# Attention steps in pairs, a later copy of the sine and cosine table, and one more empty step ahead of each batch's transforms

## The chip, the cores and the metric

The kernel runs on one core of a Trainium2 chip, in one launch. The metric is the device time of that launch in microseconds; the figure to forecast is the median of several executions. TensorE (PE in the rows) multiplies matrices, ScalarE (ACT) evaluates functions, copies and casts, VectorE (DVE) and GpSimd (POOL) work elementwise, and SyncE (SP) issues the DMAs. Each of them takes its instructions in program order.

## The reference

Three layers follow one another, in float32, over 4 batches, 448 positions and 768 features (12 heads of 64):

```python
# 1. attention with a sigmoid in place of the softmax
scores = q @ k.T / sqrt(64) - log(448)
x = sigmoid(scores) @ v                      # (4, 12, 448, 64) -> (4, 448, 768)
# 2. Fourier mixing, normalisation and a feed-forward network
u  = x + real(fft(fft(x, axis=1), axis=2))
un = (u - mean(u)) / sqrt(var(u) + 1e-6)
x  = u + relu(un @ w_ch1) @ w_ch2            # 768 -> 3072 -> 768
# 3. gated causal convolution
gate = sigmoid(conv(x, conv_w))              # 5 taps along the positions
out  = (gate * (x @ w_val)) @ w_out
```

## The kernel before

**Attention.** Heads go two at a time: 24 pairs of heads, 6 to a batch. Each pair takes four steps, one for each block of 128 keys (the fourth block, 64 keys of each head, is done for both heads in one). The main loop runs over the 96 steps `t`; `s = t % 4` is the block, `r` the step within the batch (24 to a batch). `scores(t)` (L355, L357) multiplies q and k in three matmuls (high by high, low by high, high by low halves) into one of two PSUM tiles `ps_s`; `sigmoid(t)` (L368, ScalarE) reads that tile; `values(t)` (L380, L382) multiplies its result with v in two passes and adds up in one `ps_m` tile over the four steps; `store_x` (L389, ScalarE) copies the sum out when `s == 3`.

For `s < 3` the scores of the two heads have 64 rows each and run side by side in the array: this shape is printed 64*128. Their values have 64 columns each and run side by side as 128*64. The fourth block and all other matmuls of this stage use the whole array, 128*128 (or some rows or columns less).

**Halves of q and k.** `prep_q` and `prep_k` cast the next pair's q and k (L308, ScalarE) and GpSimd subtracts for the low half (L309). Before, `prep_q` stands in the step with `s == 0` and `prep_k` in that with `s == 1`, both behind that step's sigmoid. The load of a further q or k waits until GpSimd has read the old one.

**One step.** In program order: scores of t+1, sigmoid of t, the casts, loads, then one step of each of the generators `fourier` (transforms of the batch before) and `norm` (normalisation of the one before that), a share of the step-wise weight preparation (`W_RATE` steps a step), then up to two ScalarE operations that those have queued (`drain`), then values and store of t-1. So the other matmuls stand between a scores and a values group.

**Tables.** The sine and cosine table `cs` comes in four parts through a staging tile (`cst`, tag `pm`, two buffers): its loads stand at r = 5, 6, 10, 11 of the first batch, its ScalarE copies at r = 8, 9, 14, 15. The first fold of a batch's transforms (`fold_part`, r = 19) uses the same two buffers. At r = 19 `peak_v` makes a 128x128 tile `pd` on VectorE, which a TensorE matmul (L117) reads at r = 21.

**Transforms.** `fourier(b)` starts at r = 2 of the next batch (the last batch's in the feed-forward stage). Its `main` waits some empty steps (`yield SLOT`), then `dstep` multiplies (L464, L468) the folded tiles `ph`, `pl`, and `mix` (L481) multiplies with `cs`. The yields counted before the first pair of `dstep` are 1 for b up to 2 and 4 for b = 3; before the second pair, 1.

**After attention** the feed-forward blocks `up` and `down` (L730, L753) take over; at each of their yields one step of what is left of `fourier`, `norm` and the weights is emitted. From there on nothing in the code is changed.

Of the kernel before, what the change touches and what calls it, by code (L numbers as in the profile page):

```python
# [7 lines left out]
F32 = mybir.dt.float32  # L8
# [9 lines left out]
B, H, S, D, DM, DFF = 4, 12, 448, 64, 768, 3072  # L18
# [19 lines left out]
G_EXP = -10  # L38
HALF_AT = (1, 3, 5, 6)
AHEAD = 7  # L40
LAG = 1
FOLD_AT = 18
WARM = 11
W_RATE = (1.6, 0.25, 1.25)
# [16 lines left out]
def body(tc, qd, kd, vd, w1d, w2d, cwd, wvd, wod, cdd, k12d, csd, eyed, out):  # L61
# [3 lines left out]
    def pool(stack, name, side="left"):  # L65
        return stack.enter_context(tc.tile_pool(name=name, bufs=1, side=side))
# [10 lines left out]
    wk = pool(attn, "wk")  # L77
# [211 lines left out]
    NHALF, NPAIR = 2 * B * H, B * NT  # L289
    raw, qk, st_of = {}, {}, {}  # L290
    SLOT = 1
# [10 lines left out]
    def halves_of(x, nm, n, on_v):  # L302
        h = wk.tile([128, n], F32R, tag=nm + "h", bufs=2, name=nm + "h")
        l = wk.tile([128, n], F32R, tag=nm + "l", bufs=2, name=nm + "l")
        if on_v:
            V.tensor_copy(h, x)
        else:
            A.activation(out=h, in_=x, func=AF.Copy)  # L308
        P.tensor_tensor(out=l, in0=x, in1=h.bitcast(F32), op=ALU.subtract)  # L309
        return h, l  # L310

    def prep_q(i):
        qk[i] = halves_of(raw[i][0], "q", S, i == 0)

    def prep_k(i):
        qk[i] += halves_of(raw.pop(i)[1], "k", 512, i < 3)
# [29 lines left out]
    def scores(t):  # L346
        i, s = divmod(t, 4)
        p = ps_s()
        qh, ql, kh, kl = qk[i]
        cs_ = slice(128 * s, 128 * s + 128)  # L350
        for n, (st, mv) in enumerate(((kh, qh), (kl, qh), (kh, ql))):
            if s < 3:
                for h in range(2):
                    hs = slice(64 * h, 64 * h + 64)
                    nc.tensor.matmul(p[:, h, :S], st[hs, cs_], mv[hs], start=(n == 0), stop=(n == 2))  # L355
            else:
                nc.tensor.matmul(p[:, 0, :S], st[:, cs_], mv, start=(n == 0), stop=(n == 2))  # L357
        if s == 3:
            qk.pop(i)
        sc[t] = p  # L360
# [3 lines left out]

    def sigmoid(t):
        n = width(t)
        sg = wk.tile([128, 2, S], F32, tag="sg", bufs=LAG + 2, name="sg")
        A.activation(out=sg[:, :n], in_=sc.pop(t)[:, :n, :S], func=AF.Sigmoid, scale=1.0 / math.sqrt(D), bias=logb)  # L368
        sig[t] = sg

    def values(t):
        i, s = t // 4, t % 4
        b, j = i // NT, i % NT
        if s == 0:
            xps[b, j] = ps_m()
        p, v, a = xps[b, j], vraw[b, j], sig.pop(t)
        if s < 3:
            for h in range(2):
                hs = slice(64 * h, 64 * h + 64)
                nc.tensor.matmul(p[hs, :S], v[:, s, hs], a[:, h], start=(s == 0), stop=False)  # L380
        else:
            nc.tensor.matmul(p[:, :S], v[:, s], a[:, 0], start=False, stop=True)  # L382
            vraw.pop((b, j))

    def store_x(t):
        i, s = t // 4, t % 4
        if s == 3:
            b, j = i // NT, i % NT
            A.activation(out=acc[b][:, j, PAD:], in_=xps.pop((b, j))[:, :S], func=AF.Copy)  # L389
# [10 lines left out]
    def fourier(b):  # L400
# [106 lines left out]
        def main():  # L507
            side.append(special())
            side.append(fold(0))
            while not hls or not rows:  # L510
                yield SLOT
            for _ in range(4 if b > 2 else 1):
                yield SLOT
            for c in range(2):
                yield from dstep(0, c, hls[0])
            side.append(fold(1))
            for h in range(2):
                nc.sync.dma_start(out=sp[h:6:2], in_=x[64 * h:64 * h + 1, 3:6])
            while len(hls) < 2:
                yield SLOT  # L520
            yield SLOT
            for c in range(2):
                yield from dstep(1, c, hls[1])
            while side:
                yield SLOT
            for _ in range(2 if b > 2 else 0):
                yield SLOT
            yield from mix(6, slice(64, NL, 64), add6)
            for t in range(3):
                yield from mix(128, slice(128 * t, 128 * t + 128), add(t))  # L530
# [105 lines left out]
    load_qk(3)  # L636
    nc.sync.dma_start(out=eye, in_=eyed)
    scores(0)
    mixed, cst, credit = {}, [], [0.0]
    for t in range(NHALF):  # L640
        i, g = t // 2, t % 2
        b = i // H
        r = t - b * 2 * H
        if t + 1 < NHALF:
            scores(t + 1)
        sigmoid(t)
        if t % 4 < 2 and t // 4 + 1 < NPAIR:
            (prep_k if t % 4 else prep_q)(t // 4 + 1)
        if t % 4 == 1 and t // 4 + 4 < NPAIR:
            load_qk(t // 4 + 4)  # L650
        if t % 4 == 1 and t // 4 + 2 < NPAIR:
            load_v(*divmod(t // 4 + 2, NT))
        if t == 0:
            amax_v(0, 0)
        if t % 4 == 2 and t // 4 + 1 < NPAIR:
            amax_v(*divmod(t // 4 + 1, NT))
        if r == 19:
            peak_v(b, 0)
        if r == 21:
            peak_v(b, 1)  # L660
        if r == 22:
            peak_v(b, 2)
            scale_v(b)
        if b and r == 2:
            fq.append(fourier(b - 1))
        step(fq)
        for n in range(3):
            if mixed.get(n) == 1:
                lq.append(norm(n))
            if n in mixed:  # L670
                mixed[n] += 1
        step(lq)
        if b == 0 and r in (6, 7, 8, 9):
            c, o = divmod(r - 6, 2)
            nc.sync.dma_start(out=cd[:, c, o], in_=cdd[:, c, o])
        if b == 0 and r == 12:
            nc.sync.dma_start(out=k12, in_=k12d)
        if b == 0 and r in (5, 6, 10, 11):
            c, o = divmod((5, 6, 10, 11).index(r), 2)
            cst.append(fk.tile([128, 3, 4 * NE], F32, tag="pm", bufs=2, name="cst")[:, :, :NP])  # L680
            nc.sync.dma_start(out=cst[-1], in_=csd[:, c, o])
        if b == 0 and r in (8, 9, 14, 15):
            c, o = divmod((8, 9, 14, 15).index(r), 2)
            push(out=cs[:, c, o], in_=cst.pop(0), func=AF.Copy)
        for n in range(2):
            if r == FOLD_AT + LAG + 4 * n:
                fold_part(b, n)
        if t > 6:
            credit[0] += W_RATE[0] if b == 0 else W_RATE[1] if r < 6 else W_RATE[2]
            step(wq, int(credit[0]))  # L690
            credit[0] %= 1
        drain(2 if t % 4 == 3 else 1)
        if t >= LAG:
            values(t - LAG)
            store_x(t - LAG)
    for t in range(NHALF - LAG, NHALF):
        values(t)
        store_x(t)
    drain()
    finish(wq)  # L700
    attn.close()
# [182 lines left out]
    for part, n in blocks:  # L884
        g, b = n // B, n % B
# [177 lines left out]
```

## Time and profile before

| | |
|---|---|
| Median of 3 runs | 1081.32 us (1080.78 to 1081.84) |
| Profiled execution: own time | 1081.04 us |
| Profiled execution: span | 1079.2 us |
| Mean granted TensorE clock | 0.995 of full speed |
| TensorE busy | 1058.7 us, 98% |
| VectorE, ScalarE, GpSimd busy | 739.2, 444.4, 180.3 us |
| Attention ends (last values matmul) | about 225.3 us from the span's start |

The span runs from the first to the last instruction; 1.84 us of the execution's own time lie around it. A busy TensorE is not a TensorE at its peak: the end of a matmul is modelled, so that a later start of the next one is seen in the distance between two starts, and only a long one as idle time.

### The profile page before, as it was taken

What the parts mean: (1) busy time and instruction counts of PE and PEld (TensorE: products, weight loads), DVE (VectorE), ACT (ScalarE), POOL (GpSimd) and SP (SyncE); (2) the same over time, 40 slices, a digit from 0 to 9 for tenths busy, and PEclk for the clock granted to TensorE, in tenths of its full rate; (3) what the DMA queues carried; (4) which work ended last, traced back from release to release, by engine and by line L of the source; (5) the groups of instructions that cost most, each with busy time, mean ns of one, the idle gap of its engine ahead of it and who ended that gap; (6) DMA issues with size and microseconds to landing.
All of it is one profiled execution on the core that took longest, in us unless ns stands there. A gap on an engine that the chain in (4) does not pass through costs nothing. (4 is left out here: it accounts for less than half of the span.)

```text
span 1079.2 us, 15323 instructions
## 1 busy us (share of the span) xinstructions
PE 1058.7 (98%) x5616; PEld 548.9 (51%) x5616; DVE 739.2 (68%) x2143; ACT 444.4 (41%) x686; POOL 180.3 (17%) x162
## 2 busy tenths in 40 slices
PE   9999999999899999999999999999999999999998
PEld 5345454546455555555555555555555545555554
DVE  2866999696985666667676566666666787776530
ACT  5675757732232233333233333133333374444321
POOL 3322223200020112211021122012221061000000
PEclk9999999999999999999999999999999999999999
DMA  6632432011112322223322222322222200000001
GB/s 218 211 94 88 130 97 88 11 46 45 30 30 59 83 64 69 78 60 88 89 75 72 60 74 72 89 73 60 73 71 76 60 1 1 1 35 35 35 35 69
DMA packets 34780, 74.13 MB, mean 69 GB/s; under 512 B 3940, under 2 KB 11920, under 8 KB 34704
## 3 DMA queue, kind: packets, MB, share of 16 engines
q1 hardware_dynamic: 34704, 73.15, 23.7%
q8 instruction: 44, 0.72, 0.3%
q14 instruction: 32, 0.26, 0.1%
HBM read 67.46 MB, written 5.51 MB: 68 GB/s over the span
## 5 line engine op out<-in xcount | busy, mean ns | idle before, releaser
L730 PE MATMUL ps_s<-un,w1hi 128*128 128x448 f16 x1152 | 312.8, 353 | 2.0 <-DVE hl L739 2.0
L753 PE MATMUL ps_m<-hh,w2hi 128*128 128x448 f16 x576 | 203.5, 353 | 3.6 <-DVE acc L757 2.4
L753 PE MATMUL ps_m<-hh,w2lo 128*128 128x448 f16 x576 | 203.6, 353 | 0.0
L753 PE MATMUL ps_m<-hl,w2hi 128*128 128x448 f16 x576 | 203.4, 353 | 0.0
L730 PE MATMUL ps_s<-un,w1lo 128*128 128x448 f16 x576 | 203.4, 353 | 0.0
L753 PEld LDWEIGHTS <-w2hi 128*128 128x128 f16 x1152 | 112.4, 98 | 109.4 <-issue 5.0
L730 PEld LDWEIGHTS <-w1hi 128*128 128x128 f16 x1152 | 112.9, 98 | 108.3 <-issue 4.1
L757 DVE SCALAR_TENSOR_TENSOR acc<-ps_m,rg,acc 128x448 f32<-128x448 f32 x192 | 129.1, 680 | 36.8 <-PE ps_m L753 36.6
L178 ACT ACTIVATE wabs<-w 128x384 f32<-128x384 f32 (+1 forms) x109 | 58.4, 547 | 223.9 <-DMA w<-w2d 81.1
L739 DVE SCALAR_TENSOR_TENSOR hl<-ps_s,hh 128x896 f16<-128x896 f32 x64 | 54.7, 855 | 80.0 <-ACT hh L737 79.9
L189 DVE TENSOR_SCALAR_CACHE_REDUCE wabs<-wabs 128x192 f32<-128x192 f32 (+1 forms) x234 | 74.7, 354 | 41.7 <-ACT wabs L178 40.7
L368 ACT ACTIVATE sg<-ps_s,logb 128x896 f32<-128x896 f32 x96 | 86.5, 912 | 26.8 <-PE ps_s L355 22.6
L753 PEld LDWEIGHTS <-w2lo 128*128 128x128 f16 x576 | 56.4, 98 | 53.0 <-issue 0.7
L730 PEld LDWEIGHTS <-w1lo 128*128 128x128 f16 x576 | 56.5, 98 | 52.8 <-issue 0.4
L191 DVE TENSOR_SCALAR wf<-wabs 128x192 int32<-128x192 int32 (+1 forms) x234 | 54.4, 272 | 35.6 <-POOL w1lo L230 13.2
L929 PE MATMUL ps_m<-xs,wvhi 128*128 128x448 f16 x288 | 78.0, 352 | 0.0
L197 DVE SCALAR_TENSOR_TENSOR wf<-w,wf 128x192 int32<-128x192 int32 (+1 forms) x234 | 77.3, 369 | 0.3
L737 ACT ACTIVATE hh<-ps_s 128x896 f16<-128x896 f32 x64 | 46.1, 720 | 73.6 <-PE ps_s L730 73.6
L194 DVE SCALAR_TENSOR_TENSOR wf<-w,wf 128x192 int32<-128x192 int32 (+1 forms) x234 | 74.6, 357 | 0.3
L380 PE MATMUL ps_m<-sg,v 128*64 128x448 f32 x288 | 70.3, 568 | 0.0
L810 DVE SCALAR_TENSOR_TENSOR gp<-acc,cw,gp 128x448 f32<-128x448 f32 x72 | 49.3, 685 | 20.3 <-ACT gp L808 18.4
L954 PE MATMUL ps_m<-gh,wohi 128*128 128x448 f16 x144 | 50.8, 352 | 0.0
(185 smaller groups left out, 1399.1 us busy)
## 6 DMA issues: line engine op xcount, KB each, us to landing
w<-w1d SPq DMA_DIRECT2D x42, 384.0 KB
w<-w2d SPq DMA_DIRECT2D x42, 384.0 KB
k<-kd SPq DMA_DIRECT2D x24, 256.0 KB
v<-vd SPq DMA_DIRECT2D x24, 256.0 KB
q<-qd SPq DMA_DIRECT2D x24, 224.0 KB
out<-o SPq DMA_DIRECT2D x24, 224.0 KB
w<-wvd SPq DMA_DIRECT2D x12, 384.0 KB
w<-wod SPq DMA_DIRECT2D x12, 384.0 KB
```

The source lines that it names most:

```text
L178: A.activation(out=wa, in_=z[:, :, 1].bitcast(F32), func=AF.Abs)
L189: V.tensor_scalar(out=a, in0=a, scalar1=LEAST, scalar2=None, op0=ALU.max, op1=ALU.max, accum_out=m[:, i:i + 1])
L191: V.tensor_scalar(out=f.bitcast(I32), in0=a.bitcast(I32), scalar1=0x07FFFFFF, scalar2=3, op0=ALU.bitwise_and, op1=ALU.logical_shift_left)
L194: V.scalar_tensor_tensor(out=f.bitcast(I32), in0=lo, scalar=29, in1=f.bitcast(I32), op0=ALU.logical_shift_right, op1=ALU.bitwise_or)
L197: V.scalar_tensor_tensor(out=f.bitcast(I32), in0=hi, scalar=-0x40000000, in1=f.bitcast(I32), op0=ALU.bitwise_and, op1=ALU.bitwise_or)
L368: A.activation(out=sg[:, :n], in_=sc.pop(t)[:, :n, :S], func=AF.Sigmoid, scale=1.0 / math.sqrt(D), bias=logb)
L380: nc.tensor.matmul(p[hs, :S], v[:, s, hs], a[:, h], start=(s == 0), stop=False)
L730: nc.tensor.matmul(p[:, i, :S], w[:, k, fs], u[:, k], start=(m == 0), stop=(m == 17))
L739: V.scalar_tensor_tensor(out=l[:, :nf], in0=p[:, :nf, :S], scalar=0.0, in1=h[:, :nf], op0=ALU.max, op1=ALU.subtract)
L753: nc.tensor.matmul(p[:, :S], w[:, f, js], hh[f // 2][k][:, f % 2], start=(m == 0), stop=(m == 3 * FC - 1))
L757: V.scalar_tensor_tensor(out=acc[b][:, j, PAD:], in0=p[:, :S], scalar=rg, in1=acc[b][:, j, PAD:], op0=ALU.mult, op1=ALU.add)
L929: nc.tensor.matmul(p[:, :S], w[:, k, js], u[:, k], start=(n == 0), stop=(n == 17))
```

## The change

The order of the work in the attention loop is changed. In every even step the scores of two steps (t+2 and t+3) are issued one after the other and then their two sigmoids; in every odd step the values of two steps (t-1 and t). The other matmuls of a step now stand ahead of both. `prep_q` and `prep_k` stand together in the step with `s == 0`, ahead of that step's scores. The number of sigmoid buffers goes from 3 to 4. Two of the four table loads move from r = 10, 11 to 13, 14, the copies from 8, 9, 14, 15 to 10, 11, 18, 19. Each `fourier` gets one empty step more ahead of its first pair of `dstep` (not in the last batch) and one more ahead of the second.

```diff
-LAG = 1
-        sg = wk.tile([128, 2, S], F32, tag="sg", bufs=LAG + 2, name="sg")
+        sg = wk.tile([128, 2, S], F32, tag="sg", bufs=4, name="sg")
 ...
-            for _ in range(4 if b > 2 else 1):
+            for _ in range(4 if b > 2 else 2):
                 yield SLOT
 ...
             while len(hls) < 2:
                 yield SLOT
+            yield SLOT
             yield SLOT
 ...
     scores(0)
+    scores(1)
+    sigmoid(0)
+    sigmoid(1)
 ...
-        if t + 1 < NHALF:
-            scores(t + 1)
-        sigmoid(t)
-        if t % 4 < 2 and t // 4 + 1 < NPAIR:
-            (prep_k if t % 4 else prep_q)(t // 4 + 1)
+        if t % 4 == 0 and t // 4 + 1 < NPAIR:
+            prep_q(t // 4 + 1)
+            prep_k(t // 4 + 1)
 ...
-        if b == 0 and r in (5, 6, 10, 11):
-            c, o = divmod((5, 6, 10, 11).index(r), 2)
+        if b == 0 and r in (5, 6, 13, 14):
+            c, o = divmod((5, 6, 13, 14).index(r), 2)
 ...
-        if b == 0 and r in (8, 9, 14, 15):
-            c, o = divmod((8, 9, 14, 15).index(r), 2)
+        if b == 0 and r in (10, 11, 18, 19):
+            c, o = divmod((10, 11, 18, 19).index(r), 2)
             push(out=cs[:, c, o], in_=cst.pop(0), func=AF.Copy)
 ...
-            if r == FOLD_AT + LAG + 4 * n:
+            if r == FOLD_AT + 1 + 4 * n:
                 fold_part(b, n)
 ...
         drain(2 if t % 4 == 3 else 1)
-        if t >= LAG:
-            values(t - LAG)
-            store_x(t - LAG)
-    for t in range(NHALF - LAG, NHALF):
-        values(t)
-        store_x(t)
+        if g == 0 and t + 2 < NHALF:
+            for n in (t + 2, t + 3):
+                scores(n)
+            for n in (t + 2, t + 3):
+                sigmoid(n)
+        if g:
+            for n in (t - 1, t):
+                values(n)
+                store_x(n)
```

## Rows read from the trace of the kernel before

**Rows 1.** The page, part 1: busy time, share of the span, instructions of each engine.
```profile
PE 1058.7 (98%) x5616; PEld 548.9 (51%) x5616; DVE 739.2 (68%) x2143; ACT 444.4 (41%) x686; POOL 180.3 (17%) x162
```

**Rows 2.** Busy time by stretch (start:end, length, engines, clock, DMA): three later batches, two short ones.
```profile
...
50.12:108.00 57.88, 56.85 (x316) 28.89 (x316) 38.46 (x99) 37.62 (x56) 14.53 (x12) 1.00 0.32 101
108.00:166.00 58.00, 56.74 (x317) 29.36 (x313) 55.17 (x124) 38.32 (x56) 17.13 (x13) 1.00 0.37 108
166.00:225.30 59.30, 57.57 (x318) 30.19 (x315) 50.13 (x114) 40.02 (x58) 14.40 (x11) 1.00 0.14 42
...
38.00:41.00 3.00, 3.00 (x11) 1.12 (x10) 2.67 (x8) 2.99 (x6) 1.57 (x2) 0.50 0.54 173
...
280.00:290.00 10.00, 7.44 (x29) 3.30 (x28) 9.93 (x24) 0.95 (x1) 0.41 (x1) 0.84 0.13 32
```

**Rows 3.** TensorE in order of time, one step in the loop: start, length, instruction.
```profile
11.90 0.47 PE L355 MATMUL ps_s<-qh,kh 64*128 64x448 f32 x2
12.21 0.36 PE L355 MATMUL ps_s<-qh,kl 64*128 64x448 f32 x2
12.41 0.37 PE L355 MATMUL ps_s<-ql,kh 64*128 64x448 f32 x2
12.71 0.97 PE L380 MATMUL ps_m<-sg,v 128*64 128x448 f32 x4
13.61 0.48 PE L355 MATMUL ps_s<-qh,kh 64*128 64x448 f32 x2
```

**Rows 4.** TensorE in order of time, groups of one shape behind each other.
```profile
7.00 0.37 PE L355 MATMUL ps_s<-ql,kh 64*128 64x448 f32 x2
7.21 0.38 PE L355 MATMUL ps_s<-qh,kh 64*128 64x448 f32 x2
7.41 0.38 PE L355 MATMUL ps_s<-qh,kl 64*128 64x448 f32 x2
...
222.85 1.72 PE L380 MATMUL ps_m<-sg,v 128*64 128x448 f32 x8
...
224.51 1.02 PE L382 MATMUL ps_m<-sg,v 128*128 128x448 f32 x2
```

**Rows 5.** Order of time, ScalarE, TensorE and SyncE around the table copy of r = 14.
```profile
35.18 0.52 ACT L259 ACTIVATE cs<-cst 128x384 fp32r<-128x384 f32 x1 [3.04 <-DMA cst<-csd]
...
36.27 0.47 PE L355 MATMUL ps_s<-qh,kh 64*128 64x448 f32 x2 [1.90 <-ACT sg L368]
...
29.87 0.43 SPq L681 DMA_DIRECT2D cst<-csd  x1
...
35.08 0.39 SPq L322 DMA_DIRECT2D v<-vd  x1
```

**Rows 6.** Order of time, VectorE and TensorE around the first batch's peak of v.
```profile
45.38 0.29 DVE L111 TENSOR_SCALAR pd<-eye,vt 128x128 fp32r<-128x128 f32 x1
...
47.26 0.33 PE L117 MATMUL ps_m<-pd,ones_r 128*128 128x128 f32 x1
```

**Rows 7.** Groups by line, 0 to 225.3 us: count, busy, mean ns, idle before.
```profile
L308 ACT ACTIVATE qh<-q 128x448 fp32r<-128x448 f32 x23 | 13.1, 569 | 0.0
...
L309 POOL TENSOR_TENSOR kl<-k,kh 128x512 fp32r<-128x512 f32 x24 | 31.7, 1321 | 50.7 <-ACT kh L308 48.4 <-DMA q<-qd 1.9 <-DVE kh L306 0.4
L309 POOL TENSOR_TENSOR ql<-q,qh 128x448 fp32r<-128x448 f32 x24 | 29.2, 1218 | 91.3 <-ACT qh L308 88.5 <-DVE qh L306 2.8
```

**Rows 8.** ScalarE in order of time: one copy-out of a finished pair of heads.
```profile
15.48 0.55 ACT L389 ACTIVATE acc<-ps_m 128x448 f32<-128x448 f32 x1 [1.12 <-PE ps_m L382]
```

**Rows 9.** What TensorE waited for, 0 to 225.3 us: total, times, longest.
```profile
PE ps_s L355 <- ACT sg L368: 4.9, 7, 1.9
```

**Rows 10.** Order of time, TensorE, ScalarE, VectorE: waits around the transforms, end of attention.
```profile
126.84 0.70 PE L464 MATMUL ps_m<-cd,pl 128*113 128x385 f16 x3 [0.91 <-DVE pl L436]
...
181.03 0.67 ACT L259 ACTIVATE e<-eo,st 12x452 f16<-12x452 f32 x1 [3.01 <-DVE eo L417]
...
223.11 1.08 DVE L618 TENSOR_TENSOR un<-tt,un 128x896 f16<-128x896 f32 x1
```

## The prediction

> **What bounds the kernel now.** I read the page's busy times first: TensorE is busy for 98% of the span, VectorE for 68%, ScalarE for 41% [rows 1]. Work that TensorE does not have to do, or that it does closer together, shortens the time, unless another engine sets the pace of that stretch. The change lies in the attention stage, so I looked next at that stage's batches in the view by stretch [rows 2]. TensorE is busy nearly throughout, but in the third batch (108 to 166 us) VectorE is busy for 55.17 of 58.00 us, in the fourth for 50.13 of 59.30, in the second for 38.46 of 57.88. The reader is to keep that third batch in mind. Last I read the order of time on TensorE, by the distance from one start to the next, since a late start does not show as idle time.
>
> A step [rows 3] has its three score matmuls start at 11.90, 12.21 and 12.41 and its values at 12.71: distances of 0.31, 0.20 and 0.30, in all 0.81 us for the scores; the values take until 13.61, 0.90 us; the step 1.71. Where two scores groups of the same shape stand behind each other [rows 4], the last matmul of the first (7.00) and the first of the second (7.21) both take 0.20 to 0.21. So a change of shape costs about 0.1 us at the end of a scores group and 0.1 at its start. Two values groups behind each other take 222.85 to 224.51, 1.66 us, against 2 x 0.90 = 1.80 apart.
>
> **The change part by part.**
>
> *Pairs.* A pair of heads now has eight changes of array shape, in the new order six: the scores of s = 0 and 1 stand together, and so do the values of s = 0 and 1. The other two neighbours (s = 2 and 3) differ in shape and save nothing. Two scores groups together take 0.31 + 4 x 0.20 + 0.30 = 1.41 instead of 1.62, which saves 0.21; the values save 0.14; 0.35 us for a pair of heads. The first two scores and the last two values already stand together [rows 4], so there are 23 of each: 23 x 0.35 = 8.05, which I count as **-8.1**. Other matmuls between two groups add a change of shape when both neighbours are of split shape. That was so at s = 1 and s = 3 and is now so at s = 2 and s = 3: two places of four either way, counted at nothing.
>
> The exits (0.30 instead of 0.20) [rows 3] fit what the Trainium skill states in "TensorEngine Tiling (Array Packing)", Key Properties: a change of the tiling mode drains TensorE. By that rule alone, only the drain would be saved, 46 removed changes at the 0.10 of the exit, an estimate of 4.6 us. The rows show the entry as well, and I take the rows.
>
> *Table copies.* The third load of the table was issued at 29.87, its copy began at 35.18, 5.3 us later; ScalarE waited 3.04 us for it, the sigmoid behind it came late and TensorE idled 1.90 us [rows 5]. From 38 to 41 us the granted clock was 0.50, the lower level, which costs half of those 3.0 us, 1.5: 3.4 us in all. The load now stands behind those of q, k and v at r = 13, the last of which SyncE issued at 35.08 [rows 5]: so about 35.5, and with the same 5.3 us it lands at about 40.8. ScalarE comes to the copy when the sigmoid of step 19 is done. Step 4 starts at 11.90 [rows 3]; a pair of heads takes 4 x 1.71 - 0.35 = 6.5; step 20 would start at about 38, and that sigmoid ends a little before, at about 37. So the later place does not by itself remove the wait, 3.8 us instead of 3.0. What changes is how much of it reaches TensorE: from 38.1 it has two scores (1.41) and the values of s = 2 and 3 to do (0.90, and 0.95 for the full-array group, whose row is 0.05 longer, 1.02 against 0.97; 1.85), until 41.4; the copy (0.5) and the next sigmoid (1.0) end at 42.3. That is 0.9 us idle, and 0.1 more for the second sigmoid.
>
> Next late is `pd`: VectorE finished it at 45.38 + 0.29 = 45.67 and TensorE read it at 47.26 [rows 6]. Its place in VectorE's queue is behind weight preparation that waits for DMAs, and those stand in SyncE's queue behind loads of q and k that GpSimd must free first, later than now since the casts stand behind the store. Two table loads less in the crowded stretch work the other way. I take 45.7 (45.0 to 47.5 are possible). TensorE then does this matmul 1.6 us earlier than before, with one more scores group (0.81) behind it: 2.4 us gained by then, of which five pairs of heads at 0.35 are 1.75. The table and `pd` together: **-0.6** (from -3.4, both waits gone, to +1.5).
>
> *Casts.* `prep_q` and `prep_k` now follow the copy-out of the finished pair of heads (0.55) [rows 8] on ScalarE. From the start of that copy the low half of k takes 0.55 + 0.57 (cast of q) + 1.22 + 1.32 (the two GpSimd subtractions, q first) [rows 7] = 3.66 us. The first matmul to read it comes after two scores (1.62), two values (1.66) and one matmul (0.31), 3.59 us. With the hand-overs and a weight load that can no longer be prefetched it is some 0.25 us late where nothing else stands between, and hidden where other matmuls do. Those of `fourier` and `norm` run in some 15 of the 24 pairs of heads by the order in the code; in the first batch the wait for `pd` absorbs it. Five pairs of heads are left: **+1.2** (0 to 6, 0.25 in all 24).
>
> *Empty steps.* TensorE waited 0.91 us in a transform for a low half from VectorE [rows 10]. One step ahead is worth 1.7 us, so this wait and smaller ones of the kind go: **-1.0** (0 to -1.5).
>
> *ScalarE's waits.* TensorE waited 4.9 us for sigmoids, 1.9 of them at the table [rows 9]; 3.0 are left in six waits. The largest followed ScalarE's 3.01 us wait for the transform's `eo` [rows 10]. Now two sigmoids are done ahead, and such an operation behind them has the 1.66 + 1.41 + 1.85 us of three pairs of groups, less itself and the next sigmoid: some 2.5 us of room. I take **-1.2** (0 to -3.0).
>
> *VectorE.* Against this stands that VectorE's work does not shrink. The third batch would be 2.1 us shorter (six pairs of heads), 55.9 us with 55.17 of VectorE work [rows 2]. I let a little over half of that batch's saving go: **+1.2** (0 to +4.2, the fourth batch too).
>
> *After attention.* Two empty steps more push the last of `norm`, such as the 1.08 us operation at 223.11 [rows 10], behind the start of the feed-forward blocks, and the last `fourier` starts a step or two later. There VectorE can be the bound: from 280 to 290 us it is busy for 9.93 us and TensorE for 7.44 [rows 2]. **+0.8** (-1 to +2.5).
>
> The fourth sigmoid buffer costs no time that a row shows; start and end of the loop are within the terms above.
>
> **The sum.** -8.1 - 0.6 + 1.2 - 1.0 - 1.2 + 1.2 + 0.8 = -7.7 us. The profiled execution's own time is 1081.04 us (span 1079.2 and 1.84 around it), so 1073.3; it lies 0.3 below the median of 1081.32, for which the forecast is 1073.6.
>
> **The rivals.**
>
> *VectorE takes most of it back.* If the third and fourth batch run at VectorE's pace, they keep none of their 2 x 2.1 us. What is left is the first batch (1.75 + 0.6) and the second (2.1), less the 0.8 after attention: 3.7 us, 1077.6. For it: 55.17 of 58.00 us. Against it: the fourth batch has 9 us of room, and the waits of TensorE for VectorE are short now.
>
> *The cast chain makes it slower.* In the new order a whole pair of heads lies between the copy-out and the next use of k, and the chain already fills it (3.66 against 3.59). If a queued ScalarE operation (0.67 for `e`) [rows 10] stands before the copy-out each time, some 0.6 us is lost in each of 24 pairs, 14.4 us. The other terms sum to -8.9, so it decides from 0.37 us for a pair of heads on; at 0.6 the time is 1081.3 + 5.5 = 1086.8. Against it: such an operation runs while TensorE is still at the 1.85 us of values before the copy, and ScalarE is busy for only 38.32 of 58.00 us in the fullest batches [rows 2].
>
> *The distance isn't a matter of shape.* If the extra 0.1 us belonged to every first and last matmul of a group, whatever stands beside it, standing together would save nothing; the rest sums to about -0.4 with the casts' and VectorE's terms smaller too: 1081. Two groups of one shape behind each other speak against it [rows 4].
>
> **How the numbers follow.** I give my forecast 0.63, VectorE 0.20, the casts 0.07, no effect of the shape 0.10. All the favourable bounds together would give 8.1 + 3.4 + 1.5 + 3.0 + 1.0 = 17.0 us, 1064.3; I do not expect all of them at once and set the low end at 1068.0. The high end of 1080.5 takes in VectorE's case and part of the one without effect, and leaves out the casts'. Within 0.2% (1079.2 to 1083.5) is about what a measurement of this kernel can't tell from no change. Faster than that: 0.79 (the forecast, most of VectorE's case); within it: 0.14; slower: 0.07.
>
> **What the new profile would show.** Right: scores groups of s = 0 and 1 with no 0.3 us distance between them, two values groups in 1.66 us, attention ended at about 218 us, and ScalarE's wait for `cst` still there with TensorE's idle time behind it halved. `pd` is then read almost as soon as it is made. Wrong: a TensorE wait for GpSimd at the second scores matmul of most pairs of heads (casts); VectorE full to the brim from 108 to 220 us with TensorE waiting at L464, L596 or L117 (VectorE); distances of 0.3 us inside the new pairs (shape); or an end of attention that is early and a feed-forward stage that starts no earlier, its first waits on VectorE longer by as much.

## The result and the profile after

The changed kernel takes 1091.95 us (median of 4 runs, 1090.02 to 1092.62) against 1081.05 us (4 runs, 1079.33 to 1081.84): a ratio of 1.0102, 95% interval 1.0088 to 1.0115. It is slower by about 11 us where 7.7 us less were forecast. The profiled execution's own time is 1090.02 us, its span 1088.2. Part 1 of its page, to set beside [rows 1]:

```profile
PE 1054.4 (97%) x5616; PEld 553.9 (51%) x5616; DVE 740.7 (68%) x2143; ACT 444.6 (41%) x686; POOL 184.2 (17%) x162
```

The work is the same and TensorE is even busy for 4 us less; what grew is the time in which it stands. Attention ends (first feed-forward matmul) at 227.72 us, before at 225.36; from there to the end of the span it takes 860.52 us, before 853.87. So the profiled execution lost 2.4 us in attention and 6.6 us behind it, 9.0 in all (it lies 1.9 us below the median, so some 2 of the 11 us are not in this account). The 6.6 were lost before 420 us: from the 433rd matmul of `up` on, the kernel before needs 670.28 us and this one 669.75. The batches by stretch, to set beside [rows 2] (length, then PE, PEld, DVE, ACT, POOL, clock, DMA):

```profile
52.20:109.10 56.90, 56.17 (x318) 30.87 (x316) 37.75 (x98) 37.24 (x56) 15.66 (x12) 0.98 0.36 110
109.10:168.30 59.20, 55.59 (x317) 30.93 (x317) 54.45 (x130) 37.87 (x55) 18.32 (x13) 1.00 0.35 105
168.30:227.70 59.40, 56.09 (x312) 30.51 (x309) 47.67 (x98) 39.75 (x58) 14.85 (x11) 1.00 0.12 36
49.00:53.00 4.00, 4.00 (x13) 1.53 (x14) 3.83 (x12) 0.00 (x0) 0.00 (x0) 0.50 0.38 112
240.00:250.00 10.00, 7.86 (x35) 4.23 (x35) 9.87 (x32) 2.96 (x5) 0.00 (x0) 0.83 0.16 42
```

The second batch is 1.0 us shorter than before, the third 1.2 us longer, though VectorE works no more in it. TensorE in order of time at a new pair of scores:

```profile
18.70 0.47 PE L354 MATMUL ps_s<-qh,kh 64*128 64x448 f32 x2
19.04 0.47 PE L354 MATMUL ps_s<-qh,kl 64*128 64x448 f32 x2
19.35 0.36 PE L354 MATMUL ps_s<-ql,kh 64*128 64x448 f32 x2
19.55 0.37 PE L354 MATMUL ps_s<-qh,kh 64*128 64x448 f32 x2
19.76 0.36 PE L354 MATMUL ps_s<-qh,kl 64*128 64x448 f32 x2
19.96 0.37 PE L354 MATMUL ps_s<-ql,kh 64*128 64x448 f32 x2
20.26 0.97 PE L379 MATMUL ps_m<-sg,v 128*64 128x448 f32 x4
```

Between the two groups (19.35, 19.55, 19.76) the distance is 0.20 to 0.21, as forecast; the 0.31 behind the second line (19.04 to 19.35) is that of the first reader of `kl`, which GpSimd had finished only at 18.99. Summed over TensorE's starts from 6 us to the end of attention, what the distances at changes of shape hold beyond those of one shape fell from 36.0 us (204 changes) to 28.0 us (157). The other late starts rose from 10.2 to 20.1 us. This is a reckoning, and where one draws the line between a change of shape and another late start moves each of these differences by 1 to 2 us. What TensorE waited for in attention (total, times, longest):

```profile
PE ps_s L354 <- ACT sg L367: 4.0, 4, 1.6
PE ps_s L354 <- POOL kl L308: 4.0, 8, 1.0
PE ps_m L116 <- DVE pd L110: 3.6, 1, 3.6
```

The second and third lines are new: TensorE begins at 48.62 to read a `pd` that VectorE finished at 48.56, and the clock's lower level lasts until 54 us. So is a chain through four queues at the start of the third batch; here it is in order of time, engine by engine:

```profile
112.71 0.33 SPq L297 DMA_DIRECT2D q<-qd  x1
114.32 0.33 SPq L298 DMA_DIRECT2D k<-kd  x1
114.70 0.42 SPq L321 DMA_DIRECT2D v<-vd  x1
115.17 1.42 SPq L551 DMA_DIRECT2D acc<-sp  x2
...
117.88 1.29 DVE L564 TENSOR_TENSOR tt<-tt,acc 128x448 f32<-128x448 f32 x2 [2.57 <-DMA acc<-sp]
...
125.29 0.67 ACT L258 ACTIVATE e<-eo,st 12x452 f16<-12x452 f32 x1 [4.82 <-DVE eo L416]
...
127.05 0.47 PE L354 MATMUL ps_s<-qh,kh 64*128 64x448 f32 x2 [1.64 <-ACT sg L367]
```

The same write-back in the kernel before:

```profile
107.01 1.43 SPq L551 DMA_DIRECT2D acc<-sp  x2
```

With the two empty steps (one ahead of each half of a batch's transforms), `fourier(0)` ends in step r = 1 of the third batch, whose q, k and v loads are written ahead of it; before, it ended in the last step of the second. SyncE's 257 issues stand in the order of the code. The q load leaves when GpSimd has read the old q (`ql` runs from 111.54 to 112.69), the k load when `kl` is done (112.64 to 114.29), and the write-back `acc<-sp` behind them at 115.17. VectorE stands at the norm's addition L564 for 2.57 us, ScalarE waits 4.82 us for `eo` made behind it, a sigmoid comes late, and TensorE idles 1.64 us. The same happens in the fourth batch (1.57 us at L564, 1.26 us on TensorE).

Behind attention, in order of time on VectorE and TensorE:

```profile
233.04 1.09 DVE L618 TENSOR_TENSOR un<-tt,un 128x896 f16<-128x896 f32 x1 [1.92 <-ACT un L258]
236.00 0.62 DVE L564 TENSOR_TENSOR tt<-acc 128x448 f32<-128x448 f32 x1
...
241.00 1.08 DVE L743 SCALAR_TENSOR_TENSOR hl<-ps_s,hh 128x896 f16<-128x896 f32 x1
...
242.14 0.90 PE L734 MATMUL ps_s<-un,w1hi 128*128 128x448 f16 x2 [4.04 <-DVE hl L743]
```

The last L618 of `norm(1)` begins 5.3 us past the end of attention; before, it began 2.3 us ahead of it [rows 10]. `norm(2)` begins (first L564) 8.3 us past it, before 0.2 us ahead. TensorE's idle time from attention's end to the 433rd feed-forward matmul is 15.2 us, before 7.9.

### The profile page after: what moved, and what is told of

The parts are those of the page before. It is cut to its first block, busy times and chain, and to the rows that moved or that the text cites. A ratio compares the mean times of both kernels' runs of the same rounds, so it can differ in the third digit from the quotient of the medians.

```text
span 1088.2 us, 15324 instructions
## 1 busy us (share of the span) xinstructions
PE 1054.4 (97%) x5616; PEld 553.9 (51%) x5616; DVE 740.7 (68%) x2143; ACT 444.6 (41%) x686; POOL 184.2 (17%) x162
## 4 chain that ended last, share of the span: by engine, by line
PE 79%; DVE 11%; issue 5%; DMA 2%; POOL 1%; ACT 1%; SPq 0%; ACTq 0%; POOLq 0%; DVEq 0%
PE ps_m L757 28%; PE ps_s L734 27%; PE ps_m L933 8%; PE ps_m L958 8%; PE ps_m L379 2%; PE ps_s L354 2%; PE ps_m L463 2%; DMA w<-w1d 1%; PE ps_m L480 1%; POOL kl L308 1%; DVE acc L761 1%; PE ps_m L381 1%; DVE un L582 1%; PE ps_s L356 1%; DVE gp L835 1%
## 5 line engine op out<-in xcount | busy, mean ns | idle before, releaser
L761 DVE SCALAR_TENSOR_TENSOR acc<-ps_m,rg,acc 128x448 f32<-128x448 f32 x192 | 129.7, 681 | 47.5 <-PE ps_m L757 47.2
L367 ACT ACTIVATE sg<-ps_s,logb 128x896 f32<-128x896 f32 x96 | 82.4, 911 | 51.8 <-PE ps_s L354 51.4
L379 PE MATMUL ps_m<-sg,v 128*64 128x448 f32 x288 | 66.2, 568 | 0.0
L308 POOL TENSOR_TENSOR ql<-q,qh 128x448 fp32r<-128x448 f32 x24 | 30.0, 1249 | 141.8 <-ACT qh L307 139.0
```

Of the source, the lines that this page charges most:

```text
L761: V.scalar_tensor_tensor(out=acc[b][:, j, PAD:], in0=p[:, :S], scalar=rg, in1=acc[b][:, j, PAD:], op0=ALU.mult, op1=ALU.add)
```

## The experiments

Seventeen kernels ran. A line of a diff stands against the kernel after unless said otherwise.

### Which part costs

No empty steps:

```diff
-            for _ in range(4 if b > 2 else 2):
+            for _ in range(4 if b > 2 else 1):
 ...
-            yield SLOT
             yield SLOT
             for c in range(2):
                 yield from dstep(1, c, hls[1])
```

> The changed kernel without its two extra empty steps ahead of the transforms; pairs, casts and table as changed. Theory 'empty steps': they push the last additions of the third batch's transforms and the last normalisation steps behind the start of the feed-forward blocks, where VectorE is late by 4.2 us instead of 2.1; the stalls from the end of attention to about 345 us are 20.4 us in the changed kernel and 13.1 before, so this kernel should be 5 to 7 us faster than the changed one, about 1085 us (some 1 to 2 us of waits for pl come back). Theory 'casts' (the late low half of k delays attention, and VectorE's lateness follows from that): the time stays within 2 us of the changed kernel, 1090 to 1092.

1082.99 us, ratio 1.0019 (1.0010 to 1.0028): 9.0 us of the 11 are the empty steps', more than the 5 to 7 expected. From attention's end it takes 853.56 us, as before.

The kernel before with the two empty steps alone (the same lines added):

> The kernel before with only the two extra empty steps. Theory 'empty steps': 4 to 7 us slower than before, 1085 to 1088 us, lost behind the end of attention, with a first wait for hl of about 4 us. Theory 'casts': the empty steps cost nothing without the new order, 1081 us, and the wait for pl at 126 us (0.9 us) is gone.

1094.85 us, ratio 1.0128 (1.0105 to 1.0152). Without pairs the steps cost even more, 13.6 us, about twice what I expected: in the profiled execution 5.0 in attention, where TensorE's waits for sigmoids grow from 4.9 to 9.4 us, and 9.0 behind it.

The table's loads and copies at their old steps:

```diff
-        if b == 0 and r in (5, 6, 13, 14):
+        if b == 0 and r in (5, 6, 10, 11):
 ...
-        if b == 0 and r in (10, 11, 18, 19):
+        if b == 0 and r in (8, 9, 14, 15):
```

> The changed kernel with the table's loads and copies at their old steps. Theory 'table does nothing of use': within 2 us of the changed kernel; ScalarE waits for the third part again, and the wait for pd stays. Theory 'table hurts' (its loads now stand ahead of the sixth weight load and delay VectorE's chain to pd): pd is ready 2 to 3 us earlier, 46 us instead of 48.6, and the kernel is 3 to 6 us faster than the changed one.

1091.55 us, ratio 1.0101 (1.0079 to 1.0124), no different from after. The long wait for `pd` goes, though `pd` is done only 0.5 us sooner (48.02): TensorE comes later, since the table's copy waits 4.80 us and TensorE 2.51 us for the sigmoid behind it.

The pairs alone, the casts' new place with them (the edits of the first and the third run together):

> The kernel before with the pairs alone: no empty steps, the table's loads and copies at their old steps. If the later table is worth nothing either way: 1082 to 1084 us, as with pairs and later table. If the later table caused the wait for pd (3.7 us, and half clock behind it): 1078 to 1080 us. If it helps, as the prediction had it (0.6 us and the stall at 34 us): 1084 to 1086 us.

1083.08 us, ratio 1.0020 (1.0011 to 1.0028), as with the later table. So the later table makes no difference that these runs show, and the pairs by themselves cost 2 us. By the reckoning above, changes of shape hold 27.3 us in its attention, 8.7 less than before, and the other late starts 19.9 us, 9.7 more. What TensorE waited for there:

```profile
PE ps_s L354 <- ACT sg L367: 5.3, 5, 2.3
PE ps_s L354 <- POOL kl L308: 3.2, 8, 0.7
PE ps_m L116 <- DVE pd L110: 2.1, 1, 2.1
PE ps_m L463 <- DVE pl L435: 2.0, 2, 1.7
```

Against [rows 9] and the 0.9 us for `pl` of [rows 10], the second and third lines are new and the last has grown.

### The casts and `pd`

The casts of q and k two steps earlier, behind a pair's sigmoids:

```diff
-        if t % 4 == 0 and t // 4 + 1 < NPAIR:
-            prep_q(t // 4 + 1)
-            prep_k(t // 4 + 1)
+        if t == 0:
+            prep_q(1)
+            prep_k(1)
 ...
+            if t % 4 == 2 and t // 4 + 2 < NPAIR:
+                prep_q(t // 4 + 2)
+                prep_k(t // 4 + 2)
```

> The changed kernel with the casts of q and k moved: those of the pair of heads after the next one are issued in the step with s = 2, behind its two sigmoids, so that they no longer stand between a store and the next scores. Theory 'casts': TensorE's waits for the low half of k (about 6.6 us in all) go, the loads of q and k are freed earlier, the weight loads behind them are issued about 2 us earlier, pd is ready in time and the 3.6 us wait with the slow clock behind it (6.7 us in all) shrinks to 2 us or less; attention ends at 214 to 219 us instead of 227.7 and the kernel takes 1080 to 1083 us. Theory 'empty steps' alone: the attention stage ends earlier, but VectorE is then as much later and the feed-forward stage starts no sooner: over 1087 us.

1090.92 us, ratio 1.0097 (1.0066 to 1.0127). The waits for `kl` fall to 0.4 us, and the time doesn't: `pd` still costs 3.5 us, sigmoids 4.9, and the granted clock falls in three more places (10.2 us lost by it in attention, reckoned as one minus the clock of each stretch of 10 us; after 3.5, before 1.7).

The same without empty steps, and with the matmul that reads `pd` a step later:

```diff
-        if r == 21:
+        if r == 22:
             peak_v(b, 1)
-        if r == 22:
+        if r == 23:
             peak_v(b, 2)
             scale_v(b)
```

> The kernel after without the two empty steps, with the casts of q and k moved two steps earlier behind a pair's sigmoids, and the spread of v's largest value in the step behind it (r = 22, its largest in r = 23) so that TensorE reaches it after VectorE has made pd. If the rest of the loss is the waits for kl (2.9 us) and pd (3.7 us) in the run without empty steps: 1077 to 1078 us, below the kernel before. Rival, the waits only move to the sigmoid and the spread to half clock, as when the casts alone were moved: 1081 to 1084 us.

1084.37 us, ratio 1.0034 (1.0021 to 1.0047): the rival's outcome. The scale is now made a step later too, and each batch's transforms begin with a 1.42 us wait of L463 for `ph` (68.3, 126.1 and 189.8 us); behind each of them stands a stretch at the lower clock (70 to 74, 128 to 135, 190 to 193 us).

`pd` earlier instead, without empty steps:

```diff
-        if r == 19:
+        if r == 18:
             peak_v(b, 0)
```

> The kernel without empty steps (pairs and later table kept), with the row of v's largest values (peak_row: vt and pd) a step earlier, in r = 18 right behind the last amax, ahead of that step's weight pieces on VectorE. If the 3.7 us wait for pd is VectorE's order (vt and pd stand behind 2.7 us of weight pieces): pd is made about 2.5 us sooner, the wait falls to about 1 us, and with it some of the half clock behind it goes: 1078.5 to 1080.5 us, against 1083.0 us. Rival, the wait only moves to the next thing that VectorE makes late: 1082 to 1084 us.

1081.13 us, ratio 1.0007 (0.9994 to 1.0021), 0.6 above the forecast range. Without the move the ratio was 1.0019, 1.3 us more, but the two intervals overlap, so that these two runs alone don't show a gain; the last kernel below does. In order of time, first the kernel without empty steps, then this one:

```profile
48.49 0.29 DVE L110 TENSOR_SCALAR pd<-eye,vt 128x128 fp32r<-128x128 f32 x1
...
48.83 0.33 PE L116 MATMUL ps_m<-pd,ones_r 128*128 128x128 f32 x1 [3.68 <-DVE pd L110]
```

```profile
45.85 0.99 DVE L110 TENSOR_SCALAR pd<-eye,vt 128x128 fp32r<-128x128 f32 x1
...
46.89 0.47 PE L116 MATMUL ps_m<-pd,ones_r 128*128 128x128 f32 x1 [1.73 <-DVE pd L110]
```

The wait hangs on VectorE's order: `pd` is begun 2.6 us sooner, and the wait falls by 2.0.

This and the casts together:

> As the kernel with pd a step earlier, and the casts of q and k two steps earlier behind a pair's sigmoids. If TensorE's waits for kl (2.9 us in the run without empty steps) are simply saved: 1076 to 1078.5 us. Rival, with the casts moved the stalls gather into fewer, longer ones with half clock behind them, as in the two runs before that moved the casts: 1081 to 1084 us, and no better than without that move.

1082.21 us, ratio 1.0015 (1.0003 to 1.0028), again the rival's: the waits for `kl` (0.6 us left) turn into waits for `ph`. In its attention:

```profile
PE ps_s L354 <- ACT sg L367: 4.3, 4, 1.7
PE ps_m L463 <- ACT ph L258: 3.8, 3, 1.4
PE ps_m L463 <- DVE pl L435: 2.2, 2, 1.6
```

### The empty steps: SyncE's queue

Both empty steps kept, the loads written behind the step's transform pieces:

```diff
-        if t % 4 == 1 and t // 4 + 4 < NPAIR:
-            load_qk(t // 4 + 4)
-        if t % 4 == 1 and t // 4 + 2 < NPAIR:
-            load_v(*divmod(t // 4 + 2, NT))
 ...
         step(lq)
+        (the same four lines)
```

> The kernel after, both empty steps kept, with the q, k and v loads of a step written behind the transforms' and the norm's pieces of the same step, so that SyncE issues the write-back acc<-sp ahead of loads that wait for GpSimd's ql and kl. Theory A: the waits of L564 for acc<-sp (2.6 us in batch 2, 1.6 us in batch 3) go, with them most of ScalarE's 4.8 us wait for eo and TensorE's 1.6 and 1.3 us for the sigmoid behind it; the feed-forward stage's part, about 6.6 us, stays: 1088 to 1089.5 us. Rival, the queue's order is an accident beside the true cause (VectorE simply has more to do in those steps): 1092 us, with the same stalls for eo and the sigmoid.

1087.39 us, ratio 1.0075 (1.0049 to 1.0100), a little below the forecast; against after's 1.0102 it is 2.9 us, with intervals that overlap, so that the trace has to decide. In order of time at the same place:

```profile
109.91 1.43 SPq L551 DMA_DIRECT2D acc<-sp  x2
111.75 0.34 SPq L297 DMA_DIRECT2D q<-qd  x1
...
114.28 1.27 DVE L564 TENSOR_TENSOR tt<-tt,acc 128x448 f32<-128x448 f32 x2
```

The write-back leaves ahead of the loads, L564 has no wait, ScalarE's wait for `eo` falls from 4.82 to 2.73 us, TensorE's waits for sigmoids from 4.0 to 1.6 us, and attention ends at 223.36 us, 4.4 earlier than after (1.7 of it by a shorter stretch at the lower clock) and 2.0 earlier than before. From there it still takes 863.4 us. The same move in the kernel before, where `fourier` ends a step ahead of the loads, should then do nothing:

> The kernel before with this one move of the loads. By the same reasoning no different from before, 1080 to 1081.5 us. Rival, the move helps by itself: 1076 to 1079 us; or it makes the loads late: above 1082 us.

1081.00 us, ratio 0.9995 (0.9982 to 1.0008): nothing. Nor in the kernel without empty steps and with `pd` earlier:

> The kernel without empty steps and with pd a step earlier (1081.1 us), with the loads written behind the transform pieces. Fourier's end then does not meet the loads, so if the order matters through the write-back alone: 1080 to 1082 us, no different. Rival, the loads' later place helps by itself: 1077 to 1079 us.

1081.85 us, ratio 1.0003 (0.9990 to 1.0015), against 1.0007 without the move. So the order made a difference only where the write-back meets the loads.

One empty step in place of two (one of the two lines ahead of `dstep(1, ...)` taken out):

> The kernel after with one of its two added empty steps taken out again (the one ahead of the second half's frequencies; the one ahead of the first half's stays), so that each batch's transforms end one attention step later than in the kernel before, not two. Theory A, SyncE's queue: with one step the write-back (acc<-sp, L551) is issued in the first step of the next batch, ahead of that batch's q, k and v loads, which stand in the second; VectorE's norm additions then don't wait for it in batches 2 and 3, and what is left is the last batch's end, which still falls past the end of attention: 1086 to 1089 us, with no wait of L564 for acc<-sp over 0.5 us in attention. Rival, any delay costs by its length: half of what both cost, 1087.5 us, but with that wait still there in attention at half its size (about 1.3 and 0.8 us). Rival, one step is harmless: 1083 us, as with none.

1087.76 us, ratio 1.0068 (1.0048 to 1.0087), within the theory's range and also the rival's number, so the time decides nothing. Its own two batches do: in the third the write-back still leaves behind the loads (115.29, v at 114.78; by the order of the code `fourier(0)` ends in r = 1 with one step as with two) and the norm's addition waits 2.10 us; in the fourth it leaves at 169.44, ahead of q at 175.03, and the addition has no wait. The forecast that both waits go failed for the third batch; that the wait hangs on the order in SyncE's queue did not, and a wait of half the size, the rival's sign, is seen in neither. From attention's end it takes 856.2 us.

### The empty steps: the norms' chain

Empty steps for the first two batches only (`2 if b < 2 else 1`, and the second one under `if b < 2`):

> The kernel after with the empty steps for the first two batches only; the third batch's transforms, whose end meets the end of attention, run as in the kernel before. Theory A: the feed-forward stage gets back its 6 to 7 us (from the end of attention to the end of the span 854 us, as in the run without empty steps), the waits in batches 2 and 3 stay: 1085 to 1086.5 us. Rival, the delay in the feed-forward stage comes from what attention has already lost (a queue of VectorE work carried along): from the end of attention 858 us or more, 1089 us or more.

1094.09 us, ratio 1.0146 (1.0114 to 1.0178). My theory fell: with no empty steps in the third batch's transforms, it still takes 861.9 us from attention's end. `fourier(2)` ends past attention all the same (its write-back leaves 1.2 us behind attention's end, before 4.2 ahead of it), and `norm(1)` begins its last piece 7.2 us past it, later than in after. That gave theory B, that the norms hand their lateness on, and a run with the first batch alone late:

> The kernel after with the two empty steps for the first batch alone; the second and third batches' transforms run as in the kernel before. Theory B, the norms' queue: the feed-forward stage starts late because norm(1), which moves one piece a step and fills the third batch's 24 steps exactly, ends past attention when fourier(1) ends two steps late (L618 last 5.3 us past attention's end in the kernel after, 2.3 us ahead of it in the kernel before), and norm(2) waits behind it. With the second batch on time norm(1) ends in attention again and the feed-forward stage gets back its 6.6 us: from attention's end to the end of the span 854 us, 1083 to 1086 us in all (the wait for acc<-sp in the second batch stays). Rival, any late batch costs the feed-forward stage its time by what attention hands on: 858 us or more from attention's end, 1088 us or more.

1095.77 us, ratio 1.0134 (1.0113 to 1.0155), 862.2 us from attention's end: the numbers that I had given the rival. Its order of time on VectorE says why (the last pieces of `norm(0)`, the first of `norm(1)`):

```profile
176.21 3.17 DVE L619 TENSOR_TENSOR un<-tt,un 128x896 f16<-128x896 f32 x2
179.90 0.61 DVE L565 TENSOR_TENSOR tt<-acc 128x448 f32<-128x448 f32 x1
```

In the kernel before `norm(0)`'s last piece begins at 167.08 and `norm(1)` at 171.66: already `norm(0)` all but fills a batch, and here it hands its lateness on. The chain begins one norm sooner than theory B had it. (That these two kernels, with fewer empty steps, are slower than after isn't explained by this; attention is 4.4 us longer in the second of them, with 8.5 us of waits for sigmoids against 4.0.) If it is the chain, two spare steps taken out of `norm(1)` must give the time back with all empty steps kept:

```diff
-        for _ in range(6 if b > 1 else 3):
+        for _ in range(6 if b > 1 else 1 if b else 3):
```

> The kernel after, all empty steps kept, with the three spare steps in the second batch's norm cut to one, so that norm(1) takes two steps fewer. Theory B: norm(1)'s last piece (L618) falls before attention's end again, norm(2) starts as soon as fourier(2) has ended, about 3 us past attention's end in place of 8.3 us, and from attention's end to the end of the span it takes 855 to 857.5 us: 1086.5 to 1088.5 us in all. Rival, the transforms' own lateness sets the feed-forward stage's start: 860 us from attention's end, 1091 us or more.

1088.71 us, ratio 1.0063 (1.0043 to 1.0084), 0.2 above the range, and 853.3 us from attention's end, below the 855 to 857.5 forecast, where after takes 860.5. VectorE there (attention ends at 233.64):

```profile
229.46 1.08 DVE L618 TENSOR_TENSOR un<-tt,un 128x896 f16<-128x896 f32 x1
235.49 0.62 DVE L564 TENSOR_TENSOR tt<-acc 128x448 f32<-128x448 f32 x1
```

`norm(1)` begins its last piece 4.2 us ahead of attention's end, and TensorE's idle time behind it falls from 15.2 to 9.7 us. This run alone doesn't prove the chain: attention itself is 5.9 us longer than after's, which gives VectorE that much more time, and counted from the span's start `norm(2)` begins only 0.5 us sooner (235.49 against 236.00). Of the 5.9 us, 5 are lost at the lower clock (8.5 against 3.5). The shorter norm also has a price of its own: its matmuls now come to `tt` before VectorE has made it (2.7 us at L569, which is new, and 2.0 at L596, where after has 0.6).

### Both cures

The whole change with the loads moved and `norm(1)` shorter:

> The kernel after, whole, with both cures: the q, k and v loads written behind a step's transform pieces, and two spare steps fewer in norm(1). If the two queues are all that the empty steps cost: attention as with the first cure (end at about 223.4 us), the rest as with the second (853.3 us): 1077.5 to 1079.5 us, below the kernel before. Rival, the two cures reach the same loss, or half clock takes it back: 1083 us or more.

1082.21 us, ratio 1.0007 (0.9996 to 1.0017), between my range and the rival's. Each cure still does its part (852.5 us from attention's end, no wait for the write-back), but attention ends at 230.1 us and not at 223.4. `pd` costs 4.4 us there, 0.8 more than with the first cure alone; the shorter norm's matmuls wait 4.1 us in place of 0.6; and 6.8 us in place of 1.7 are lost at the lower clock, at or behind these waits (total, times, longest; of the first, 1.2 us stand behind attention):

```profile
PE ps_m L116 <- DVE pd L110: 5.6, 3, 4.4
PE ps_m L596 <- DVE tt L587: 4.1, 2, 2.3
```

With `pd` a step earlier as well:

> The same with v's row of largest values (vt, pd) a step earlier, in r = 18. In the kernel without empty steps this saved 1.9 us; if it adds, 1.5 to 2 us less than with both cures: 1075.5 to 1078 us. Rival, the wait moves on: no different from both cures.

1079.11 us, ratio 0.998 (0.997 to 0.999), the one version below the kernel before, and 3.1 us below both cures, with intervals apart, where 1.5 to 2 were forecast. Attention ends at 222.09 us, and from there it takes 854.20 us. This is what shows the chain: attention ends 1.3 us sooner here than with the loads alone moved (223.36), so VectorE had no more time, and what follows is 9.2 us shorter (863.4). `norm(2)` begins 1.9 us past attention's end in place of 8.3. The move of `pd` doesn't account for that, since without empty steps it left the time behind attention as it was (853.55 and 853.56 us). The stretch from 40 to 60 us, first with both cures, then with `pd` too:

```profile
40.00:60.00 20.00, 14.65 (x67) 6.21 (x63) 18.36 (x50) 10.43 (x16) 4.42 (x4) 0.83 0.50 145
```

```profile
40.00:60.00 20.00, 17.21 (x91) 7.73 (x88) 18.44 (x49) 13.43 (x21) 4.74 (x5) 1.00 0.63 193
```

The wait of 4.4 us has become 1.7, and in this execution the clock stays at its upper level: 91 matmuls against 67 in the same 20 us. This is one execution of each kernel, the slowest of twelve with both cures. Over all twelve the median of the mean granted clock is 0.9945 with both cures and 0.995 with `pd` earlier, which is about 0.5 us of the span, so the lower clock accounts for little of the 3.1 us between their medians; how the rest divides up stays open.

## Why the prediction was wrong

**Pairs.** The -8.1 was right within the reckoning: 8.0 us fewer in the profile after, 8.7 in the pairs alone. The rows' reading, exit and entry, held. By the drain alone, an estimate from what the Trainium skill states in "TensorEngine Tiling (Array Packing)", Key Properties, it would have been 4.6 us.

**Casts, VectorE's and ScalarE's waits.** +1.2, +1.2 and -1.2 were to leave 6.9 us of the pairs' gain. The pairs alone cost 2 us, so this is the first step that failed: I priced the waits of the old order, and not those that an earlier TensorE runs into. The casts took 4.0 us in eight waits (3.2 in the pairs alone), 0.5 each where I had 0.25 in five; `pd` and `pl` are made no sooner than before, and TensorE waits for them (3.6 us for `pd`; 2.1 for `pd` and 2.0 for `pl` in the pairs alone). ScalarE's waits did not go: TensorE's waits for sigmoids fell only from 4.9 to 4.0 us. (The room of 2.5 us that I gave a queued ScalarE operation comes to 3.25 by its own terms, 4.92 less 0.67 and 1.0; ScalarE's wait of 4.82 us for `eo` overran it.) VectorE's pace isn't it: the third batch takes 59.2 us with 54.45 of VectorE work in it. That the waits move when one of them is taken away is shown by the two kernels without empty steps whose casts are early (`kl` into `ph`). How much each wait is worth by itself stays open, since it depends on whether the lower clock follows.

**Table and `pd`.** The wait for the table stayed (2.99 us, forecast 3.8) and TensorE's idle time at it fell from 1.90 to 0.70 us, forecast 0.9. But `pd` was done at 48.56 us where I took 45.7 and allowed 47.5 at most. With the half clock behind it (48.6 to 54 us, half of 5.4) the places cost 0.70 + 3.64 + 2.7 = 7.0 us against 1.90 + 1.7 before (from 37.6 to 41 us; I had counted 1.5): -0.6 became some +3.4. I had named the path, VectorE's chain of weight preparation behind loads in SyncE's queue, and mis-sized it. In the trace the delay stands at the third load of q that waits for GpSimd, in the second pair of heads, first before, then after:

```profile
15.60 0.33 SPq L298 DMA_DIRECT2D q<-qd  x1
41.15 0.95 DVE L181 TENSOR_SCALAR wabs<-w 128x256 int32<-128x256 int32 x1 [0.33 <-DMA w<-w1d]
```

```profile
17.79 0.33 SPq L297 DMA_DIRECT2D q<-qd  x1
43.28 0.29 DVE L180 TENSOR_SCALAR wabs<-w 128x256 int32<-128x256 int32 x1 [0.86 <-DMA w<-w1d]
```

The second line of each is the last piece in VectorE's order ahead of `pd` that waits for a weight load. Both are 2.1 to 2.2 us later, of the 2.9 us of `pd`. So the casts' new place seems to delay `pd` through SyncE's queue as well; with the casts two steps earlier that load left at 16.85 and `pd` was done 1.0 us sooner, but no run tests this path by itself. Undoing the table alone gives nothing back, since the stall at the table then returns.

**Empty steps.** -1.0 and, after attention, +0.8: this is the step with the largest error. They cost 9.0 us (13.6 alone). I counted `fourier`'s instructions and not its last two DMAs, which move past the loads of the next batch in SyncE's queue; and I saw that the last of `norm` goes behind attention's end, but priced it as one 1.08 us operation. It is the end of a chain in which each norm all but fills a batch (23 of 24 steps by the order of the code), and two steps late at its head are two steps late at its end, where `norm(2)` then starts 8.5 us later against attention's end. All nineteen kernels line up by that start: where `norm(2)` begins 1.9 us past attention's end or sooner, it takes 852.2 to 854.2 us from there; at 2.8 us (one empty step) 856.2; at 8.0 us or later 858.9 to 863.4. The benefit that I forecast came: in attention the waits for `pl` are gone after (0.9 us before; 1.9 without empty steps).

**The rivals.** None had this mechanism. The range's upper end took in what I had priced, and the two costs that decided were not among them. Of the views named as signs of being wrong, two came in part: the wait for GpSimd at the second scores matmul, in eight pairs of heads and not in most, and first waits on VectorE in the feed-forward stage that are longer (4.0 us for `hl` against 2.0), though with no early end of attention. Of those named as signs of being right, the distances inside the pairs came, and `pd` read as soon as it is made (48.56, 48.62), though TensorE had waited 3.6 us for it by then.

## What to carry to other kernels

A step that is delayed moves all that it issues: follow its DMAs into the issuing queue, and look at what stands ahead of them there and at which release that waits for. Where pieces are handed out one per step, count the steps that the chain needs against those that it has; a chain without slack carries a delay to the end of the stage. A gain on the busiest engine is kept only as far as the values that it waits for are made sooner too: list them, with the time at which each is done, before counting the gain.

## What the runs showed of the hardware

VectorE's scalings (TENSOR_SCALAR) take longer when they begin beside one of GpSimd's subtractions. `pd` took 0.29 us where no subtraction was running at its start, 0.99 us at 45.85 with GpSimd's `ql` running from 45.62 to 46.75, and 1.10 us in the last kernel:

```profile
45.67 1.13 POOL L308 TENSOR_TENSOR ql<-q,qh 128x448 fp32r<-128x448 f32 x1 [6.48 <-ACT qh L307]
45.78 1.10 DVE L110 TENSOR_SCALAR pd<-eye,vt 128x128 fp32r<-128x128 f32 x1
```

Both times `pd` ends 0.08 to 0.09 us behind the subtraction (46.84 against 46.75, 46.88 against 46.80). So it looks held up until GpSimd is done, and not slowed by a factor. The scalings of 128x256 int32 in attention show the same: alone 0.29 us; begun beside a subtraction, 0.38 to 1.37 us in the kernels before, after and last, each ending 0.15 to 0.18 us behind it. So the place of the casts bears on VectorE's pace as well.

A TensorE stall of 1.7 us before the same matmul went with the lower clock in one kernel (`pd` earlier without empty steps: 0.78 from 40 to 50 us, the lower level setting in during the stall) and not in another (the last one, 1.00). Which stalls bring it on, these runs do not settle; the mean granted clock differs between executions of one kernel too (0.993 to 0.998 in the last one).
